# The second feed-forward in the list schedule, its tiles in the buffers of w_out

## The chip, the cores and the metric

The kernel runs on one core of a Trainium2 chip, as one launch. The metric is the device time of that launch in microseconds. Engines are named as the profile names them: PE is TensorE (PEld its weight loads), DVE VectorE, ACT ScalarE, POOL GpSimd, SP SyncE, which here issues all DMAs.

## What is computed

Windowed attention (4 sequences of 576 tokens, 8 heads of 64, window 64), then a feed-forward with squared ReLU, then a second one with a softmax-weighted activation and a layer norm without bias. The attention's output is 2304 tokens of width 512.

```python
def _moe_ref(x, w_in, w_out):                  # 512 -> 2048 -> 512
    h = np.maximum(x @ w_in, 0.0)
    return (h * h @ w_out).astype(np.float32)

def _moe2_ref(x, w_in, w_out, g_ln):           # 512 -> 1024 -> 512
    h = x @ w_in
    e = np.exp(h - np.max(h, axis=-1, keepdims=True))
    solu = h * (e / (np.sum(e, axis=-1, keepdims=True) + 1e-09))
    mu, var = np.mean(solu, axis=-1, ...), np.mean((solu - mu) ** 2, axis=-1, ...)
    ln = (solu - mu) / np.sqrt(var + 1e-06) * g_ln
    return (ln @ w_out).astype(np.float32)
```

## The kernel before

Every fp32 operand of the large products is split into a high and a low part that TensorE takes, and a product is three matmuls per block (`TERMS`, line 22). The weights arrive as 64-bit floats and are taken apart by DVE and ACT (`weights`, lines 196 to 240).

The first part (lines 175 to 524) works through the tokens in five passes of 8, 6, 8, 6 and 8 blocks of 64 (`PASSES`, line 124). Each pass needs the attention of its blocks, which is spread over the pass before it, and goes through 16 chunks of the 2048 hidden columns. Of chunk kk a pass does a product of 12 matmuls into one bank of `ps_a` (`product`, line 402, in the rows `ps_h L402`), then relu and square on ACT, the exact square on POOL, the low part on DVE (`rest`, line 418, the tile `g`), and 12 matmuls that add the chunk to the pass's sums (`second`, line 428, `ps_y`). The sums of 512 tokens fill four banks: two tiles of `ps_b`. I write y14 and y15 for the last two of these accumulations in the last pass. Behind them DVE and ACT copy the sums out (lines 449 and 451), and SP stores them to `x2_dram`. In the last pass the 16 weight tiles of the second feed-forward replace those of w_in one by one.

The order of all engines in this part is made ahead by `Plan` (lines 25 to 90): every step is a task with an engine, an estimated duration, a rank, the tasks it comes after, and the buffers that it takes and gives back. `run` puts next the task that can start first by its estimates, and among those with one start the lowest rank; the tasks are then written out in the order of their planned starts. Each engine works through its own row in that order.

The second part (lines 527 to 618) stands behind the plan and is written in a plain loop, whose order on the engines the framework settles. Of each of 18 tiles of 128 tokens it loads x from `x2_dram` (`load_x`), splits it into high (ACT, line 544) and low (DVE, line 545), does 24 matmuls h = x w_in into a pair of banks of `ps_b` (`mm_h`, line 555), then on DVE the maximum (560), on ACT the exponential (563), on DVE the scaling (567), the statistics (570, 572) and the centring (576), on POOL the root (575). `mm_t` transposes the result on PE (587) and splits it on ACT (588) and DVE (589); `mm_o` does 24 matmuls with the second weights (599), ACT scales the sums (602), SP stores them. I write h(i), transposes(i) and o(i) for these steps of tile i. In the loop o follows h by two tiles and the transposes by one:

```python
        for i in range(NTT + 2):
            if i < NTT:
                mm_h(i)
                ...
            if 0 <= i - 2 < NTT:
                mm_o(i - 2)
            if 0 <= i - 1 < NTT:
                mm_t(i - 1)
```

PSUM has eight banks: `ps_b` two pairs, `ps_a` two, and two of `ps_t` (scores and attention in the first part, transposes in the second).

Of the kernel before, what the change touches and what calls it, by code (L numbers as in the profile page):

```python
# [93 lines left out]
def kernel(  # L94
# [79 lines left out]

    with ExitStack() as c1:
# [14 lines left out]
        plan = Plan({"raw": RAWS, "wm": WMB, "qk": 1, "v": 1, "e": 2, "pt": 1, "t": 2, "b": 2, "a": 2, "r": 2, "g": 3})  # L190
# [334 lines left out]


    with ExitStack() as c2:
        s_p = c2.enter_context(tc.tile_pool(name="s", bufs=2))
# [1 line left out]
        NTT = NT // P  # L530
        sol, lnT, rst = {}, {}, {}
        x2 = {}

        def load_x(i):
            xr = s_p.tile([P, DC, P], F32, tag="xr", name="xr")
            nc.sync.dma_start(out=xr, in_=x2_dram[:, :, i * P : i * P + P])
            x2[i] = xr

        x2s = {}

        def split_x(i):
            xr = x2.pop(i)
            xx = s_p.tile([P, 2, DC, P], F32R, tag="xx", name="xx")
            S.activation(out=xx[:, 0], in_=xr, func=AF.Copy)
            V.tensor_tensor(out=xx[:, 1], in0=xr, in1=xx[:, 0].bitcast(F32), op=ALU.subtract)
            x2s[i] = xx

        def mm_h(i):
            xx = x2s.pop(i)
            ps = ps_b.tile([P, 2, 512], F32, tag="b", name="ps_h2")  # L550
            for hf in range(NH2):
                n = 0
                for c in range(DC):
                    for wi, xi in TERMS:
                        T.matmul(ps[:, hf, :], xx[:, xi, c, :], w2i[hf * DC + c][:, wi, :],  # L555
                                 start=n == 0, stop=n == 3 * DC - 1)
                        n += 1
            h = ps.rearrange("p a b -> p (a b)")
            nmax = s_p.tile([P, 1], F32, tag="nmax2", name="nmax2")
            V.tensor_reduce(out=nmax, in_=h, axis=AX.X, op=ALU.max, negate=True)  # L560
            e = s_p.tile([P, DFF2], F32, tag="e2", name="e2")
            sums = s_p.tile([P, 1], F32, tag="sums2", name="sums2")
            S.activation(out=e, in_=h, func=AF.Exp, bias=nmax, accum_out=sums)
            rs = s_p.tile([P, 1], F32, tag="rs2", name="rs2")
            V.tensor_scalar(out=rs, in0=sums, scalar1=1e-9, scalar2=None, op0=ALU.add)
            V.reciprocal(rs, rs)
            V.scalar_tensor_tensor(out=e, in0=e, scalar=rs, in1=h, op0=ALU.mult, op1=ALU.mult)
            bn = s_p.tile([P, NH2, 6], F32, tag="bn", name="bn")
            for hf in range(NH2):
                V.bn_stats(out=bn[:, hf, :], in_=e[:, hf * 512 : hf * 512 + 512])  # L570
            mv = s_p.tile([P, 2], F32, tag="mv", name="mv")
            V.bn_aggr(out=mv, in_=bn.rearrange("p a b -> p (a b)"))
            rstd = s_p.tile([P, 1], F32, tag="rstd", name="rstd", bufs=4)
            V.tensor_scalar(out=rstd, in0=mv[:, 1:2], scalar1=1e-6, scalar2=None, op0=ALU.add)  # L574
            G.tensor_tensor(out=rstd, in0=rstd, in1=mhalf, op=ALU.pow)  # L575
            V.tensor_scalar(out=e, in0=e, scalar1=mv[:, 0:1], scalar2=None, op0=ALU.subtract)
            sol[i] = e
            rst[i] = rstd

        def mm_t(i):  # L580
            e = sol.pop(i)
            l = s_p.tile([P, 2, KF2, P], F32R, tag="lnT", name="lnT")
            for hf in range(KF2 // 4):
                ps = ps_t.tile([P, 4, P], F32, tag="t", name="ps_lt")
                for u in range(4):
                    kk = 4 * hf + u
                    T.transpose(ps[:, u, :], e[:, kk * P : kk * P + P], ident)  # L587
                S.activation(out=l[:, 0, 4 * hf : 4 * hf + 4, :], in_=ps, func=AF.Copy)  # L588
                V.tensor_tensor(out=l[:, 1, 4 * hf : 4 * hf + 4, :], in0=ps,  # L589
                                in1=l[:, 0, 4 * hf : 4 * hf + 4, :].bitcast(F32), op=ALU.subtract)  # L590
            lnT[i] = l

        def mm_o(i):
            l = lnT.pop(i)
            ps = ps_a.tile([P, 512], F32, tag="a", name="ps_o")
            n = 0
            for kk in range(KF2):
                for wi, xi in TERMS:
# [62 lines left out]
```

## Time and profile before

| | |
|---|---|
| median of three runs | 728.3 us (727.86 to 731.81) |
| the profiled execution | 728.8 us |
| its span, first to last instruction | 726.7 us |
| PE busy | 697.0 us (96%), 4630 instructions |
| PEld busy | 605.5 us (83%) |
| DVE, ACT, POOL busy | 371.5, 307.9, 139.0 us |
| granted PE clock, mean | 0.988 of full speed |

Matmuls overlap each other, so PE's busy time says where it had work, not how fast it went. The pace is read from the start of one group to the start of the next in the chain that ended last, and a stall from the idle time before an instruction in the timeline. The granted clock is 1.00 at 2.4 GHz and 0.50 at 1.2 GHz.

### The profile page before, as it was taken

The page shows a single profiled execution, that of the slowest core. Times are in us where ns is not written, and L with a number is a line of the kernel's source. Part 1 is how long each engine was busy: PE and PEld are TensorE (multiplying, and loading weights), DVE is VectorE, ACT ScalarE, POOL GpSimd, SP SyncE. Part 2 cuts the span into 40 slices and gives each one's busy share as a digit, 9 for nine tenths or more (in the row PEclk, how much of TensorE's full clock was granted, in tenths as well). Part 3 has the DMA queues.
Part 4 walks back from the last instruction along what each step waited for, and adds up shares of the span by engine and source line. Part 5 has one row for each costly group of instructions (what it writes and reads, how often), then busy time and mean ns, then how long its engine had stood idle before and what let it go on. Part 6 is the DMA issues. An engine that isn't in the chain of part 4 may idle for free.

```text
span 726.7 us, 11758 instructions
## 1 busy us (share of the span) xinstructions
PE 697.0 (96%) x4630; PEld 605.5 (83%) x4630; DVE 371.5 (51%) x678; ACT 307.9 (42%) x755; POOL 139.0 (19%) x161
## 2 busy tenths in 40 slices
PE   6687999999999999999999999998999999999997
PEld 3677888999999888788999988886888888888876
DVE  3999999522333221322223166555675646665561
ACT  5776767334445233433434243455323231323132
POOL 2122332412223122222222121121010011010100
PEclk9889999999999999999999999999999999999999
DMA  7766644012222211212111062222211011110001
GB/s 225 252 203 227 212 151 147 31 38 87 66 66 67 73 36 30 63 40 86 39 66 60 1 206 99 89 85 66 80 44 58 30 45 44 59 39 35 14 30 43
DMA packets 34565, 60.51 MB, mean 83 GB/s; under 512 B 5072, under 2 KB 16336, under 8 KB 34512
## 3 DMA queue, kind: packets, MB, share of 16 engines
q1 hardware_dynamic: 34512, 59.78, 24.7%
q8 instruction: 36, 0.59, 0.3%
q14 instruction: 17, 0.14, 0.1%
HBM read 50.34 MB, written 9.44 MB: 82 GB/s over the span
## 4 chain that ended last, share of the span: by engine, by line
PE 81%; DVE 11%; issue 2%; DMA 2%; ACT 2%; SPq 0%; POOL 0%; ACTq 0%; DVEq 0%
PE ps_h L402 24%; PE ps_y L428 23%; PE ps_h L555 14%; PE ps_o L599 14%; DVE wm L215 3%; PE ps_lt L587 2%; DVE wm L220 2%; PE ps_v L350 2%; PE ps_s L294 2%; PE ps_p L327 1%; DVE wm L210 1%; DVE wa L231 1%; DVE g L418 1%; DVE wb L231 1%; DMA qk<-in_k 1%
## 5 line engine op out<-in xcount | busy, mean ns | idle before, releaser
L402 PE MATMUL ps_h<-x,wa 128*128 128x256 f32 (+2 forms) x1152 | 220.5, 344 | 4.3 <-DVE wa L231 2.5
L428 PE MATMUL ps_y<-g,wb 128*128 128x256 f32 (+2 forms) x1152 | 219.6, 343 | 5.2 <-DVE g L418 5.0
L428 PEld LDWEIGHTS ps_y<-g,wb 128*128 128x128 f32 x1152 | 188.2, 190 | 26.2 <-DVE g L418 7.1
L402 PEld LDWEIGHTS ps_h<-x,wa 128*128 128x128 f32 x1152 | 190.4, 194 | 23.1 <-DVE wa L231 3.4
L415 POOL TENSOR_TENSOR r<-r 128x256 f32<-128x256 f32 (+2 forms) x96 | 84.0, 877 | 305.3 <-ACT g L412 288.3
L418 DVE TENSOR_TENSOR g<-r,g 128x256 fp32r<-128x256 f32 (+2 forms) x96 | 55.0, 580 | 152.0 <-POOL r L415 147.6
L408 ACT ACTIVATE r<-ps_h 128x256 f32<-128x256 f32 (+2 forms) x96 | 46.9, 489 | 157.6 <-PE ps_h L402 153.4
L555 PE MATMUL ps_h<-w2i,xx 128*128 128x512 f32 x432 | 104.9, 393 | 0.4 <-ACT y L449 0.4
L599 PE MATMUL ps_o<-w2o,lnT 128*128 128x512 f32 x432 | 104.5, 391 | 0.8 <-ACT lnT L588 0.5
L599 PEld LDWEIGHTS ps_o<-w2o,lnT 128*128 128x128 f32 x432 | 80.7, 188 | 17.9 <-ACT lnT L588 0.8
L555 PEld LDWEIGHTS ps_h<-w2i,xx 128*128 128x128 f32 x432 | 79.9, 188 | 17.0 <-ACT y L449 0.8
L309 ACT ACTIVATE e<-e,nmax 128x128 f32<-128x128 f32 (+1 forms) x144 | 55.0, 384 | 38.4 <-DVE nmax L305 38.4
L602 ACT ACTIVATE o<-ps_o,rstd 128x512 f32<-128x512 f32 x18 | 12.4, 689 | 111.8 <-PE ps_o L599 109.9
L575 POOL TENSOR_TENSOR rstd<-rstd,mhalf 128x1 f32<-128x1 f32 x18 | 16.8, 935 | 192.5 <-DVE rstd L574 192.5
L412 ACT ACTIVATE g<-r 128x256 fp32r<-128x256 f32 (+2 forms) x96 | 50.3, 524 | 5.1 <-PE ps_y L428 2.3
L318 POOL TENSOR_TENSOR e<-e,sums 128x512 f32<-128x512 f32 (+1 forms) x36 | 37.0, 1031 | 73.2 <-DVE sums L315 61.9
L560 DVE TENSOR_REDUCE nmax<-ps_h 128x1 f32<-128x1024 f32 x18 | 21.9, 1218 | 43.9 <-PE ps_h L555 43.9
L301 DVE SCALAR_TENSOR_TENSOR e<-ps_s,mask 128x512 f32<-128x512 f32 (+1 forms) x36 | 23.5, 653 | 38.9 <-PE ps_s L294 38.9
L589 DVE TENSOR_TENSOR lnT<-ps_lt,lnT 128x512 fp32r<-128x512 f32 x36 | 23.3, 683 | 36.3 <-ACT lnT L588 36.3
L220 DVE SCALAR_TENSOR_TENSOR wm<-wraw,wm 128x512 int32<-128x512 int32 x48 | 36.3, 757 | 1.2
L215 DVE SCALAR_TENSOR_TENSOR wm<-wraw,wm 128x512 int32<-128x512 int32 x48 | 35.1, 731 | 1.3
L206 ACT ACTIVATE wm<-wraw 128x512 f32<-128x512 f32 x48 | 31.5, 664 | 2.3 <-DMA wraw<-in_w_out 1.7
(57 smaller groups left out, 511.9 us busy)
## 6 DMA issues: line engine op xcount, KB each, us to landing
wraw<-in_w_in SPq DMA_DIRECT2D x24, 512.0 KB, 3.8
wraw<-in_w_out SPq DMA_DIRECT2D x24, 512.0 KB, 3.3
vt<-in_v SPq DMA_DIRECT2D x32, 256.0 KB, 2.9
kt<-in_k SPq DMA_DIRECT2D x16, 384.0 KB, 4.2
xr<-x_dram SPq DMA_DIRECT2D x18, 256.0 KB, 3.1
out<-o SPq DMA_DIRECT2D x18, 256.0 KB, 2.0
qt<-in_q SPq DMA_DIRECT2D x17, 256.0 KB, 2.8
x_dram<-y SPq DMA_DIRECT2D x12, 256.0 KB, 2.5
```

Source lines behind the costliest of these rows:

```text
L215: V.scalar_tensor_tensor(out=t, in0=o["raw"][:, :, 1], scalar=-0x80000000, in1=t, op0=ALU.bitwise_and, op1=ALU.bitwise_or)
L220: V.scalar_tensor_tensor(out=t, in0=o["raw"][:, :, 0], scalar=29, in1=t, op0=ALU.logical_shift_right, op1=ALU.bitwise_or)
L309: S.activation(out=o["er"][:, a, w], in_=o["er"][:, a, w], func=AF.Exp, bias=o["nmax"][:, a, w : w + 1], accum_out=o["sums"][:, a, w : w + 1])
L318: G.tensor_tensor(out=o["er"][:, a], in0=o["er"][:, a], in1=o["sums"][:, a].unsqueeze(2).to_broadcast([P, HP, W]), op=ALU.mult)
L402: T.matmul(ps[:, :N], wa[kk][:, wi, c * P : c * P + P], xs[t][:, xi, c, n0:n1], start=n == 0, stop=n == 3 * DC - 1)
L408: S.activation(out=o["r"], in_=o["h"][:, :N], func=AF.Relu)
L412: S.activation(out=o["g"][:, 0, :N], in_=o["r"], func=AF.Square)
L415: G.tensor_tensor(out=o["r"], in0=o["r"], in1=o["r"], op=ALU.mult)
L418: V.tensor_tensor(out=o["g"][:, 1, :N], in0=o["r"], in1=o["g"][:, 0, :N].bitcast(F32), op=ALU.subtract)
L428: T.matmul(acc[t][d // 2][:, d % 2, n0:n1], wb[kk][:, wi, d * P : d * P + P], o["g"][:, xi, :N], start=kk == 0 and n == 0 and n0 == 0, sto ...
L555: T.matmul(ps[:, hf, :], xx[:, xi, c, :], w2i[hf * DC + c][:, wi, :], start=n == 0, stop=n == 3 * DC - 1)
L599: T.matmul(ps, l[:, xi, kk, :], w2o[kk][:, wi, :], start=n == 0, stop=n == 3 * KF2 - 1)
```

## The change

The second feed-forward's steps become tasks of the plan, in one function per tile (`tile2`), so they share ranks and buffers with the last pass. The arithmetic and the sizes of the instructions are those of before, but for a product h(i), which is planned in two halves of 12 matmuls, and o(i), likewise. Its tiles (x, its split, the exponential, the split transposes, the result) take buffers of `wb_p`, 16 tiles that held w_out and that the last pass gives back one by one (`"wb": 0`, `gone`). The sums of the last pass lie in one tile of `ps_b` and the two banks of `ps_t`, so that a pair of `ps_b` is free for h(0). `x2_dram` becomes one tensor per pass, so that a load of x waits for its own pass's stores only. The last product of the last pass gets a lower rank, and the last tiles' o a higher one. The line numbers of the new program differ: L431 is y, L537 h, L575 the transposes, L590 o, L526 and L529 the split of x, L454 and L456 the copies of the sums.

```diff
-    x2_dram = dram.tile([P, DC, NT], F32, name="x2_dram")
+    x2_dram = [dram.tile([P, DC, n * BLK], F32, name=f"x2_dram{t}") for t, n in enumerate(PASSES)]
...
-        plan = Plan({..., "r": 2, "g": 3})
+        plan = Plan({..., "r": 2, "g": 3, "wb": 0})
...
-                    acc[t] = [ps_b.tile([P, 2, 512], F32, tag="b", name="ps_y") for _ in range(2)]
+                    acc[t] = [ps_b.tile([P, 2, 512], F32, tag="b", name="ps_y") for _ in range(1 if t == LAST else 2)]
+                    acc[t] = [a[:, i] for a in acc[t] for i in range(2)]
+                    if t == LAST:
+                        acc[t] += [ps_t.tile([P, 512], F32, tag="t", name="ps_y") for _ in range(2)]
...
-            i = add("PE", mm(N), rank, product, [ready["a", kk], *done], take=["a"])
+            i = add("PE", mm(N), rank - 6 * (last and t == LAST), product, [ready["a", kk], *done], take=["a"])
...
-            p = add("PE", mm(N), rank + 4.5, second, [e, ready["b", kk], before], take=["b", "b"] if first else [], give=["g"])
+            gone = ["wb"] * (t == LAST)
+            p = add("PE", mm(N), rank + 4.5, second, [e, ready["b", kk], before], take=[] if not first else ["b", "t", "t"] if t == LAST else ["b", "b"],
+                    give=["g", *gone])
...
+        def spare(dtype, name):
+            return wb_p.tile([P, 2, 512], dtype, tag="wb", name=name)
+
+        def tile2(i, rank, rank_o):
...
+            a = add("SP", 1.0, rank - 14, load_x, stored[t] + h_of.get(i - 3, []), take=["wb"], late=2.0)
+            a = add("ACT", 0.62, rank - 6, x_high, [a], take=["wb"])
+            a = add("DVE", 0.62, rank - 6, x_low, [a], port=True, give=["wb"])
+            for hf in range(NH2):
+                a = add("PE", mm(512), rank, lambda hf=hf: mm_h(hf), [a, *(ready["2i", hf * DC + c] for c in range(DC))],
+                        take=["b"] * (hf == 0), give=["wb"] * (hf == 1))
+            h_of[i] = [a]
+            a = add("DVE", 1.17, rank, max_h, [a])
+            a = add("ACT", 1.33, rank, exp_h, [a], take=["wb"])
+            a = add("DVE", 1.45, rank, solu, [a], give=["b"])
+            a = add("DVE", 1.50, rank, stats, [a])
+            r = add("POOL", 1.05, rank, root, [a])
+            a = add("DVE", 0.62, rank, centered, [a], port=True)
+            p = add("PE", 0.95, rank + 6, transposes2, [a], take=["t", "t"], give=["wb"])
+            ls = []
+            for hf in range(2):
+                a = add("ACT", 0.60, rank, lambda hf=hf: t_high(hf), [p], take=["wb"])
+                ls.append(add("DVE", 0.66, rank, lambda hf=hf: t_low(hf), [a], give=["t"]))
+            for hf in range(2):
+                a = add("PE", mm(512), rank_o, lambda hf=hf: mm_o(hf),
+                        [a if hf else None, ls[hf], *(ready["2o", 4 * hf + c] for c in range(4))], take=["a"] * (hf == 0), give=["wb"])
+            a = add("ACT", 0.72, rank_o, scaled, [a, r], take=["wb"], give=["a"])
+            add("SP", 1.0, rank_o, store_o, [a], late=2.0, give=["wb"])
+
+        NTT, TILE = NT // P, 4 * mm(512) + 1.2
+        for i in range(NTT):
+            at = begin[-1] + TILE * i
+            tile2(i, at, at + TILE * (1.5 + 0.6 * max(0, i - (NTT - 5))))
...
-    with ExitStack() as c2:
-        s_p = c2.enter_context(tc.tile_pool(name="s", bufs=2))
-        ps_t = c2.enter_context(tc.tile_pool(name="ps_t2", bufs=2, space=PSUM))
...
```

The order of the engines is the same in both programs up to the last pass. PE before, from the last product of the last pass (L402) over y14 and y15 (L428, 24 in one row) into the second feed-forward:

```order
L402 MATMUL ps_h<-x,wa 128x512 x12
L428 MATMUL ps_y<-g,wb 128x512 x24
L555 MATMUL ps_h_5103<-w2i,xx 128x512 x24
L555 MATMUL ps_h_5151<-w2i,xx 128x512 x24
L555 MATMUL ps_h_5214<-w2i,xx 128x512 x24
L587 MATMUL ps_lt<-ident,e_5130 128x128 x8
L555 MATMUL ps_h_5305<-w2i,xx 128x512 x21
L599 MATMUL ps_o<-w2o,lnT 128x512
L555 MATMUL ps_h_5305<-w2i,xx 128x512 x3
L599 MATMUL ps_o<-w2o,lnT 128x512 x23
L587 MATMUL ps_lt<-ident,e_5178 128x128 x8
```

PE now, the same place:

```order
L402 MATMUL ps_h<-x,wa 128x512 x12
L431 MATMUL ps_y<-g,wb 128x512 x12
L537 MATMUL ps_h_5073<-w2i,xx 128x512 x12
L431 MATMUL ps_y<-g,wb 128x512 x12
L537 MATMUL ps_h_5073<-w2i,xx 128x512 x12
L537 MATMUL ps_h_5130<-w2i,xx 128x512 x24
L537 MATMUL ps_h_5177<-w2i,xx 128x512 x12
L575 MATMUL ps_lt<-ident,e_5147 128x128 x8
L537 MATMUL ps_h_5177<-w2i,xx 128x512 x12
L590 MATMUL ps_o<-w2o,lnT 128x512 x12
L575 MATMUL ps_lt<-ident,e_5197 128x128 x8
L590 MATMUL ps_o<-w2o,lnT 128x512 x36
```

Half of h(0) has moved ahead of y15. Each later h is in two halves with the transposes of the tile before it in between, and o follows at once, a tile earlier than it did; the pattern of four rows (h half, transposes, h half, o) repeats from tile 4 to tile 15.

ACT before, from the last relu and square of the last pass (L408, L412) over the last two weight tiles (L206, L227, L228) to the copies of the sums (L449):

```order
L408 ACTIVATE r<-ps_h 128x512
L412 ACTIVATE g<-r 128x512
L227 ACTIVATE wm<-wm,gcol 128x512
L544 ACTIVATE xx<-xr 128x512
L228 ACTIVATE w2o<-wm 128x512
L206 ACTIVATE wm<-wraw 128x512
L544 ACTIVATE xx<-xr 128x512
L227 ACTIVATE wm<-wm,gcol 128x512
L228 ACTIVATE w2o<-wm 128x512
L449 ACTIVATE y<-ps_y 128x512 x2
```

ACT now, the same place:

```order
L408 ACTIVATE r<-ps_h 128x512
L412 ACTIVATE g<-r 128x512
L227 ACTIVATE wm<-wm,gcol 128x512
L228 ACTIVATE w2o<-wm 128x512
L206 ACTIVATE wm<-wraw 128x512
L227 ACTIVATE wm<-wm,gcol 128x512
L228 ACTIVATE w2o<-wm 128x512
L454 ACTIVATE y<-ps_y 128x512 x2
L549 ACTIVATE e_5147,sums_5148<-ps_h_5073,nmax_5143 128x1024
```

The copies that split x are gone from here; they stand with their DVE halves early in the last pass (tiles 0 to 2) or behind the exponentials.

PE before, the end, from the transposes of tile 15:

```order
L587 MATMUL ps_lt<-ident,e_6424 128x128 x8
L599 MATMUL ps_o<-w2o,lnT 128x512 x13
L587 MATMUL ps_lt<-ident,e_6515 128x128 x4
L599 MATMUL ps_o<-w2o,lnT 128x512 x11
L587 MATMUL ps_lt<-ident,e_6515 128x128 x4
L599 MATMUL ps_o<-w2o,lnT 128x512 x12
L587 MATMUL ps_lt<-ident,e_6604 128x128 x4
L599 MATMUL ps_o<-w2o,lnT 128x512 x12
L587 MATMUL ps_lt<-ident,e_6604 128x128 x4
L599 MATMUL ps_o<-w2o,lnT 128x512 x24
```

PE now, the end, from the transposes of tile 14:

```order
L575 MATMUL ps_lt<-ident,e_6409 128x128 x8
L537 MATMUL ps_h_6437<-w2i,xx 128x512 x12
L537 MATMUL ps_h_6484<-w2i,xx 128x512 x24
L590 MATMUL ps_o<-w2o,lnT 128x512 x12
L575 MATMUL ps_lt<-ident,e_6499 128x128 x8
L590 MATMUL ps_o<-w2o,lnT 128x512 x12
L537 MATMUL ps_h_6584<-w2i,xx 128x512 x12
L575 MATMUL ps_lt<-ident,e_6542 128x128 x8
L537 MATMUL ps_h_6584<-w2i,xx 128x512 x12
L590 MATMUL ps_o<-w2o,lnT 128x512 x36
L575 MATMUL ps_lt<-ident,e_6645 128x128 x8
L590 MATMUL ps_o<-w2o,lnT 128x512 x36
```

The last transposes are no longer split into fours, and o of tiles 14 to 16 is kept back to stand behind the transposes of the next tile.

## Rows read from the trace of the kernel before

**Rows 1.** Stages (us): busy of PE, PEld, DVE, ACT, POOL; clock, DMA, GB/s.

```profile
0.00:100.00 100.00, 79.18 (x807) 67.53 (x808) 85.74 (x169) 69.81 (x207) 25.52 (x39) 0.93 0.64 214
100.00:498.60 398.60, 397.03 (x2793) 355.57 (x2793) 157.68 (x286) 171.28 (x432) 95.61 (x103) 1.00 0.22 71
498.60:508.80 10.20, 7.59 (x25) 5.43 (x23) 5.33 (x10) 5.91 (x10) 1.04 (x1) 0.83 0.40 120
508.80:722.80 214.00, 213.21 (x1008) 176.93 (x1008) 122.73 (x216) 60.22 (x106) 16.83 (x18) 1.00 0.13 43
722.80:726.70 3.90, 0.00 (x0) 0.00 (x0) 0.00 (x0) 0.69 (x1) 0.00 (x0) 0.90 0.18 67
...
703.00:705.00 2.00, 1.24 (x6) 0.65 (x5) 1.23 (x2) 2.00 (x4) 0.00 (x0) 1.00 0.35 131
```

**Rows 2.** The same view, the two stretches behind the gap at the seam.

```profile
504.00:506.00 2.00, 1.95 (x5) 1.57 (x6) 2.00 (x4) 0.27 (x1) 0.00 (x0) 0.51 0.43 125
506.00:508.00 2.00, 2.00 (x7) 1.61 (x6) 1.43 (x3) 1.07 (x2) 0.00 (x0) 0.63 0.44 130
```

**Rows 3.** Timeline of PE at the seam: start, us, instruction, [idle before <-releaser].

```profile
498.63 3.19 PE L428 MATMUL ps_y<-g,wb 128*128 128x512 f32 x13
504.05 4.37 PE L428 MATMUL ps_y<-g,wb 128*128 128x512 f32 x11 [2.23 <-DVE g L418]
508.82 16.60 PE L555 MATMUL ps_h<-w2i,xx 128*128 128x512 f32 x72 [0.40 <-ACT y L449]
```

**Rows 4.** Timeline of the other engines at the seam.

```profile
498.87 7.21 SPq L536 DMA_DIRECT2D xr<-x_dram  x4
...
500.23 1.04 POOL L415 TENSOR_TENSOR r<-r 128x512 f32<-128x512 f32 x1 [4.48 <-ACT g L412]
502.04 0.63 ACT L544 ACTIVATE xx<-xr 128x512 fp32r<-128x512 f32 x1 [1.27 <-DMA xr<-x_dram]
...
502.70 0.69 DVE L545 TENSOR_TENSOR xx<-xr,xx 128x512 fp32r<-128x512 f32 x1 [3.84 <-ACT xx L544]
...
503.31 0.68 DVE L418 TENSOR_TENSOR g<-r,g 128x512 fp32r<-128x512 f32 x1
...
509.06 0.68 DVE L231 TENSOR_TENSOR w2o<-wm,w2o 128x512 fp32r<-128x512 f32 x1
```

**Rows 5.** The chain that ended last: start, us, what.

```profile
493.26 2.79 PE ps_y L428 x12
...
537.19 0.87 PE ps_lt L587 x8
...
549.64 4.80 PE ps_h L555 x21
...
573.24 4.80 PE ps_h L555 x21
```

**Rows 6.** Timeline of DVE in the first tiles of the second feed-forward.

```profile
514.58 1.23 DVE L560 TENSOR_REDUCE nmax<-ps_h 128x1 f32<-128x1024 f32 x1 [4.83 <-PE ps_h L555]
...
517.46 1.28 DVE L567 SCALAR_TENSOR_TENSOR e<-e,rs,ps_h 128x1024 f32<-128x1024 f32 x1
...
532.09 1.21 DVE L560 TENSOR_REDUCE nmax<-ps_h 128x1 f32<-128x1024 f32 x1
...
538.50 1.29 DVE L589 TENSOR_TENSOR lnT<-ps_lt,lnT 128x512 fp32r<-128x512 f32 x2 [3.64 <-ACT lnT L588]
...
540.47 1.28 DVE L567 SCALAR_TENSOR_TENSOR e<-e,rs,ps_h 128x1024 f32<-128x1024 f32 x1
...
543.42 0.74 DVE L576 TENSOR_SCALAR e<-e,mv 128x1024 f32<-128x1024 f32 x1
```

**Rows 7.** Timeline early in the last pass, PE and ACT.

```profile
426.78 2.95 PE L428 MATMUL ps_y<-g,wb 128*128 128x512 f32 x12
...
432.57 0.60 ACT L408 ACTIVATE r<-ps_h 128x512 f32<-128x512 f32 x1 [0.27 <-PE ps_h L402]
```

**Rows 8.** Timeline of PE, its last instructions.

```profile
717.09 5.70 PE L599 MATMUL ps_o<-w2o,lnT 128*128 128x512 f32 x24
```

More of the change, by code (lines that the diff above doesn't have):

```diff
@@ L127 @@
     ORDER = FIRSTS + [j for j in range(NB) if j % blocks_per_seq]
-    HALF, BEHIND = len(FIRSTS), 6
+    HALF, BEHIND, LAST = len(FIRSTS), 6, len(PASSES) - 1
     assert sum(PASSES) == NB and PASSES[0] == 2 * HALF and HALF % 2 == 0
@@ L179 @@
         g_p = c1.enter_context(tc.tile_pool(name="g", bufs=3))
+        s_p = c1.enter_context(tc.tile_pool(name="s", bufs=2))
         ps_t = c1.enter_context(tc.tile_pool(name="ps_t", bufs=2, space=PSUM))
@@ L189 @@
         assert all(n % 2 == 0 for n in PASSES) and blocks_per_seq % 2
[L190 removed]
+        plan = Plan({"raw": RAWS, "wm": WMB, "qk": 1, "v": 1, "e": 2, "pt": 1, "t": 2, "b": 2, "a": 2, "r": 2, "g": 3, "wb": 0})
         add = plan.add
@@ L385, in attention @@
             x_ready[n] = add("DVE", 0.65, rank, rest, [h], give=["b" if alone else "t"])
-        acc, in_of, out_of = {}, {}, {}
+        acc, in_of, out_of, stored = {}, {}, {}, {}
         def mm(N):
@@ L448, in evict @@
                         if d % 2:
-                            S.activation(out=y[:, :n1], in_=acc[t][d // 2][:, d % 2, :n1], func=AF.Copy)
+                            S.activation(out=y[:, :n1], in_=acc[t][d][:, :n1], func=AF.Copy)
                         else:
-                            V.tensor_copy(y[:, :n1], acc[t][d // 2][:, d % 2, :n1])
+                            V.tensor_copy(y[:, :n1], acc[t][d][:, :n1])
                     def store(d=d):
-                        at = starts[t] * BLK
-                        nc.sync.dma_start(out=x2_dram[:, d, at : at + n1], in_=o["y", d][:, :n1])
-                    y = add("ACT" if d % 2 else "DVE", 0.62, rank, evict, [p] + ys[-1:] * (d % 2), take=["wm"], give=["b"] * (d % 2))
+                        nc.sync.dma_start(out=x2_dram[t][:, d], in_=o["y", d][:, :n1])
+                    y = add("ACT" if d % 2 else "DVE", 0.62, rank, evict, [p] + ys[-1:] * (d % 2), take=["wm"],
+                            give=["t"] if t == LAST and d > 1 else ["b"] * (d % 2))
                     ys.append(y)
-                    add("SP", 1.0, rank, store, [y], late=2.0, give=["wm"])
+                    stored.setdefault(t, []).append(add("SP", 1.0, rank, store, [y], late=2.0, give=["wm"]))
         PAIR0, PAIR = 13.0, 6.6
@@ L524 @@
             plan.emit()
-    with ExitStack() as c2:
-        s_p = c2.enter_context(tc.tile_pool(name="s", bufs=2))
-        ps_t = c2.enter_context(tc.tile_pool(name="ps_t2", bufs=2, space=PSUM))
[L530 to L598, printed above, removed]
-                    T.matmul(ps, l[:, xi, kk, :], w2o[kk][:, wi, :], start=n == 0, stop=n == 3 * KF2 - 1)
-                    n += 1
-            o = s_p.tile([P, DM], F32, tag="o", name="o")
-            S.activation(out=o, in_=ps, func=AF.Copy, scale=rst.pop(i))
-            nc.sync.dma_start(out=out[i * P : i * P + P, :], in_=o)
-        load_x(0)
-        load_x(1)
-        split_x(0)
-        for i in range(NTT + 2):
-            if i < NTT:
-                mm_h(i)
-                if i + 1 < NTT:
-                    split_x(i + 1)
-                if i + 2 < NTT:
-                    load_x(i + 2)
-            if 0 <= i - 2 < NTT:
-                mm_o(i - 2)
-            if 0 <= i - 1 < NTT:
-                mm_t(i - 1)
```

73 lines of the change are left out of this document (70 added, 3 removed).

## The prediction

> **What bounds the kernel now.** I read the stages first. TensorE is the engine that ends last, and its idle time lies in four places [rows 1]: 20.8 us in the first 100 us, 1.6 us in the next 398.6, 2.6 us in the 10.2 us between the two feed-forwards, and 0.8 us in the 214.0 us of the second one. Behind its last matmul come 3.9 us of eviction and store. The order of all engines is the same in both programs until the last pass (its weights' split on VectorE and ScalarE, the first x load on SP's queue), so the 20.8 us and the 1.6 us stay, and so do the last 3.9 us. What can move is the seam and the second feed-forward.
>
> At the seam TensorE starts the accumulation of the last chunk but one (y14) at 498.63 and the first product of the second feed-forward at 508.82 [rows 3]: 10.19 us. Two accumulations take 2.79 us each at the pace before it [rows 5], 5.58 in all, so the seam loses **4.61 us**, more than the 2.6 us of idle time. The rest is the clock: behind the gap the granted clock is 0.51 for 2 us and 0.63 for 2 more [rows 2], the lower level (1.2 GHz) for most of it. That is 2 x 0.49 + 2 x 0.37 = 1.7 us. The cause stands in the queues: y15 waits for VectorE's g, and VectorE stood 3.84 us at the split of x, which waits for ScalarE's copy, which waits for the x load that SP issued at 498.87 and that let ScalarE start at 502.04 [rows 4]. POOL had the square ready at 500.23 + 1.04 = 501.27 [rows 4]; g ran at 503.31 all the same.
>
> The second feed-forward runs at 11.80 us a tile (two periods of the chain are 573.24 - 549.64 = 23.60) [rows 5]. 18 tiles are 212.4 us. It takes from 508.82 to 717.09 + 5.70 = 722.79 [rows 3, 8], 213.97 us: **1.57 us** over the dense time, 0.76 of it idle at 703 to 705 [rows 1], the rest the split transposes of the last tiles.
>
> **The change, part by part.**
>
> *The seam.* By the order, half of h(0) (12 matmuls, half of 24, 2.73 us) now stands between y14 and y15, the other half behind y15. The x splits of tiles 0 to 2 have left this place, so g15 follows POOL's 501.27 and is done near 501.3 + 0.7 = 502.0. TensorE comes to y15 at 498.63 + 2.79 + 2.73 = 504.15: 2.1 us of cover. Behind y15 and the second half, at 504.15 + 2.79 + 2.73 = 509.7, stands h(1), which takes the bank pair of y's first half and so waits for VectorE's and ScalarE's evictions. What those two engines do from g15 to the last eviction took, in the trace, from 503.31 to 509.06 + 0.68 = 509.74 [rows 4], waits included; begun at 501.3 it ends by 507.7. It is hidden by 2 us. The second bank pair is free, since the last pass keeps half its sums in the scores' banks; that is what lets tile 0 start early. So the whole 4.61 us should go: -4.61, and at the least the idle 2.6 if the clock fell without a gap, which no row suggests.
>
> *The x loads and splits in the last pass.* Three loads and three splits now stand in the last pass, with SP's queue waiting ahead of weight loads: the first load for y0's end (its buffer is w_out's first), the second for VectorE's first split. ScalarE's first copy waits for y1, 426.78 + 2.79 = 429.6 [rows 7], and the load has then had 5 us where one took 3.2 (498.87 to 502.04) [rows 4]. Behind it on ScalarE are one weight scaling, one rounding and the relu that ran at 432.57 [rows 7]: 2.9 us for three pieces of some 0.6 to 0.7. The weights that SP holds back are needed only at the seam, 70 us later. Cost 0; if a load were 3 us late the relu would slip and the accumulation behind it might wait 1 us, once. Range 0 to 1.
>
> *The tiles in the steady stretch.* The order is now h(i) first half, transposes(i-1), h(i) second half, o(i-1), for i from 4 to 15. The chain behind a product is: maximum to the start of the scaling 517.46 - 514.58 = 2.88; scaling to the end of the centring 543.42 + 0.74 - 540.47 = 3.69 [rows 6]; with 0.2 before it (h(0) ends near 508.82 + 16.60/3 = 514.35 [rows 3]) and 0.1 behind, 6.9 us. TensorE meanwhile does o (24) and half an h (12): at 11.80 less 0.87 for the transposes [rows 5], 36/48 of 10.93 = 8.20 us. Slack 1.3 us. The maximum must also find VectorE free: the split of the transposes ends 538.50 + 1.29 - 537.19 = 2.6 us after they start [rows 5, 6], and TensorE takes 0.87 + 2.73 = 3.60 from there to the end of h. So 11.80 us a tile as before: 0. In the old order three groups of 24 lay over the same chain, so this slack is much thinner than it was.
>
> *The first and the last tiles.* VectorE has tiles 0 and 1 on top of each other. Followed by hand with the same durations: centring of tile 0 ends at 516.5, maximum of 1 at 517.7, the x split at 518.4, scaling of 1 at 520.8, two splits of tile 0's transposes at 522.1, centring of 1 at 524.5. TensorE comes to the transposes of tile 1 at 509.7 + 5.47 + 2.73 + 0.87 + 2.73 + 2.73 = 524.2: a wait of 0.3. At the end: h(16) ends 5.47 after h(15); its centring follows tile 15's on VectorE and ends some 14.8 after h(15), where TensorE is there at 14.5: 0.3. Transposes of tile 17 have 36 matmuls over their chain (8.2 against 6.9), and o(17) has half of o(16) over its splits. So the 1.57 us of before becomes 0.6: **-1.0**; bounds 0 and -1.57.
>
> *The new buffers.* Tiles of the second feed-forward take w_out's buffers, 16 of them, six a tile. Behind the first three loads and splits, at least 85 matmuls and transposes stand in TensorE's order between the last reader of a buffer and the instruction that takes it; a tile has 56. Cost 0.
>
> **Sum.** -4.61 - 1.57 + 0.6 = -5.6 us. Against the profiled execution, 726.7 of span and 728.8 in all: 721.1 and 723.2. The median of the runs shown is 728.3, 0.5 under the profiled one, so I forecast **722.7 us**, 0.8% less. About 0.5% (3.6 us, 724.7) is what a measurement can tell from no change.
>
> **The rivals.**
>
> *The gain comes in part.* The waits at the transposes of tiles 1 and 16 are short by my reckoning, but either may drop the clock as the gap from 501.82 (498.63 + 3.19) to 504.05 did [rows 3]. Each would cost the 1.7 us of [rows 2], 3.4 for both: 726.1, no measurable change. Against it: the 0.76 us of idle time at 703 to 705 left the clock at 1.00 there [rows 1]. The Trainium skill (TensorE: Matmul & The Clock Gate, A second HAM failure mode: psum-queue depth-cycling) tells of a kernel that cycled PSUM banks and micro-idled so often that its clock kept falling; by that rule the new order, with its thinner slack, would go this way. The trace disagrees so far as it goes: the old second feed-forward cycles the same banks at 1.00 throughout [rows 1]. The same time comes out if a late load or late evictions at the seam give back 3 us. Chance 0.15.
>
> *The chain behind each product is longer than its cover.* The mechanism is the thin slack: if exp stands in ScalarE's queue behind something that waits (an x copy for its load, an o copy for its matmuls), every tile's transposes wait. The trace has it: from the maximum at 532.09 to the end of the centring at 544.16 tile 3 took 12.07 us [rows 6], harmless under the old cover. With 0.3 around it that is 12.4, 4.2 over the 8.20; 12 tiles make 50 us, less 5.6: 773 us. It decides from 1.3 + 5.6/12 = 1.8 us of stretch, and is slower by over 0.5% from 2.1. Against it: in the new order exp stands directly behind the copies of the preceding transposes, which with VectorE's part are done 1 us before the product ends (2.6 against 3.60). Chance 0.05.
>
> **How the numbers follow.** Forecast 0.80 (721.6, no wait at all and half a microsecond of scatter, to 724.6), partial 0.15 (724.7 to 727), slower 0.05. The range 721.4 to 725.6 leaves out the slow rival, the upper half of the partial one and some scatter below. Faster 0.80, same 0.14, slower 0.06 (the rest is scatter of the runs).
>
> **What would show it.** In the profile of the changed kernel: between y14 and y15 12 matmuls of the second feed-forward and no gap over 0.3 us; the granted clock at 1.00 from 498 to the end; 18 tiles at 11.80 with waits of TensorE for the centring of under 1 us in all; the last matmul ends about 717.2. The forecast is wrong if TensorE waits at the transposes in the steady stretch, if y15 or h(1) waits, or if what lies before the last pass has moved.

## The result and the profile after

The changed kernel takes 723.28 us (median of 5 runs, 722.17 to 724.17), the kernel before, run beside it, 729.49 us (727.86 to 731.81): a ratio of 0.9909 [0.9881, 0.9938], 0.6 to 1.2% faster. The forecast was 722.7 us in 721.4 to 725.6. The profiled execution has a span of 720.3 us against 726.7 before, where the working gave 721.1.

The stages of the new trace, cut at the same events as [rows 1] (columns as there: busy time of PE, PEld, DVE, ACT, POOL, then clock, DMA share, GB/s):

```profile
497.90:508.10 10.20, 10.20 (x46) 8.30 (x45) 5.14 (x9) 5.49 (x9) 1.04 (x1) 1.00 0.09 33
508.10:716.50 208.40, 208.30 (x989) 172.95 (x987) 123.77 (x213) 60.42 (x104) 16.98 (x18) 1.00 0.14 44
...
504.00:506.00 2.00, 2.00 (x11) 1.58 (x10) 0.88 (x2) 1.05 (x2) 0.00 (x0) 1.00 0.04 12
506.00:508.00 2.00, 2.00 (x10) 1.67 (x9) 1.01 (x2) 1.09 (x2) 0.00 (x0) 1.00 0.37 137
```

The 10.2 us at the seam, of which TensorE was busy for 7.59 at a mean clock of 0.83 [rows 1], are now busy throughout at 1.00. The two stretches that showed 0.51 and 0.63 [rows 2] show 1.00. From there to the last matmul 0.1 us of idle time is left.

TensorE's timeline at the seam, which answers to [rows 3] (L431 is the accumulation, L537 the first product of the second feed-forward, L575 the transposes):

```profile
497.90 2.96 PE L431 MATMUL ps_y<-g,wb 128*128 128x512 f32 x12
500.69 2.90 PE L537 MATMUL ps_h<-w2i,xx 128*128 128x512 f32 x12
503.43 2.95 PE L431 MATMUL ps_y<-g,wb 128*128 128x512 f32 x12
506.22 11.06 PE L537 MATMUL ps_h<-w2i,xx 128*128 128x512 f32 x48
517.12 1.04 PE L575 MATMUL ps_lt<-ident,e 128*128 128x128 f32 x8
```

No group has a wait behind it. y14, half of h(0), y15, and then the rest of h(0), h(1) and half of h(2) stand edge to edge: from the start of y14 to the transposes of tile 0 are 19.22 us, where 2 x 2.79 and 60 products of the steady pace (5.47 / 24 each) make 19.25.

The other engines there, which answer to [rows 4]:

```profile
499.50 1.04 POOL L415 TENSOR_TENSOR r<-r 128x512 f32<-128x512 f32 x1 [4.48 <-ACT g L412]
500.58 0.69 DVE L418 TENSOR_TENSOR g<-r,g 128x512 fp32r<-128x512 f32 x1 [2.44 <-POOL r L415]
...
505.73 1.28 DVE L456 COPY y<-ps_y 128x512 f32<-128x512 f32 x2
...
506.44 1.09 ACT L454 ACTIVATE y<-ps_y 128x512 f32<-128x512 f32 x2 [1.36 <-DVE y L456]
```

VectorE now stands idle ahead of g15 and follows POOL by 0.04 us (499.50 + 1.04 = 500.54). g15 ends at 501.27, y15 starts at 503.43. The four evictions end at 506.44 + 1.09 = 507.53; h(1) starts about 506.22 + 2.73 = 508.95.

In the chain that ended last (start, us, what), one row of a steady tile and the same row ten tiles later:

```profile
544.54 2.73 PE ps_h L537 x12
...
662.61 2.73 PE ps_h L537 x12
```

That is 118.07 / 10 = 11.81 us a tile; [rows 5] gave 11.80. What the chain of one steady tile has to spare is seen in the timeline of DVE and PE at tile 4 (its centring, then its transposes):

```profile
556.84 0.74 DVE L567 TENSOR_SCALAR e<-e,mv 128x1024 f32<-128x1024 f32 x1
...
558.92 1.04 PE L575 MATMUL ps_lt<-ident,e 128*128 128x128 f32 x8
```

The centring ends at 557.58, TensorE comes at 558.92: **1.34 us of slack** (1.25 to 1.34 at tiles 3 to 15). At tile 16, where two centrings follow each other, the centring ends at 694.48 + 0.74 = 695.22 and the transposes start at 695.38. The products ahead of them, the transposes and TensorE's last group, which answers to [rows 8]:

```profile
692.43 2.88 PE L537 MATMUL ps_h<-w2i,xx 128*128 128x512 f32 x12
695.38 1.07 PE L575 MATMUL ps_lt<-ident,e 128*128 128x128 f32 x8
...
708.02 8.45 PE L590 MATMUL ps_o<-w2o,lnT 128*128 128x512 f32 x36
```

From the start of these 12 products to the transposes are 2.95 us, where the pace is 2.73: TensorE waits 0.22 us for the centring here, which the timeline doesn't mark because the products' modelled ends overlap what follows.

For the experiments I use one length, **M**: from the start of y14 to the end of the last matmul. Before it was 717.09 + 5.70 - 498.63 = 224.16 us [rows 3, 8], now it is 708.02 + 8.45 - 497.90 = 218.57: 5.59 less. The other 0.8 of the 6.4 us that the span lost are 0.1 behind the last matmul and 0.73 ahead of y14, which started at 498.63 before and at 497.90 here. The seven runs below have the code of the new kernel up to g15, or nearly, and start y14 between 498.63 and 499.92, so these 0.73 us are scatter of the beginning and not of the change.

### The profile page after: what moved, and what is told of

The parts are those of the page before. It is cut to its first block, busy times and chain, and to the rows that moved or that the text cites. A ratio compares the mean times of both kernels' runs of the same rounds, so it can differ in the third digit from the quotient of the medians.

```text
span 720.3 us, 11740 instructions
## 1 busy us (share of the span) xinstructions
PE 693.0 (96%) x4630; PEld 602.2 (84%) x4630; DVE 373.4 (52%) x678; ACT 309.6 (43%) x755; POOL 139.6 (19%) x161
## 4 chain that ended last, share of the span: by engine, by line
PE 85%; DVE 10%; issue 2%; DMA 1%; ACT 1%; SPq 1%; DVEq 0%; ACTq 0%
PE ps_y L431 25%; PE ps_h L402 24%; PE ps_h L537 14%; PE ps_o L590 14%; DVE wm L215 2%; PE ps_lt L575 2%; PE ps_v L350 2%; PE ps_s L294 2%; PE ps_p L327 1%; DVE wm L220 1%; PE ps_warm L640 1%; DVE wm L210 1%; DVE wb L231 1%; DVE wa L231 1%; DMA wraw<-in_w_out 1%
## 5 line engine op out<-in xcount | busy, mean ns | idle before, releaser
L402 PE MATMUL ps_h<-x,wa 128*128 128x256 f32 (+2 forms) x1152 | 218.3, 341 | 5.0 <-DVE wa L231 2.9
L431 PE MATMUL ps_y<-g,wb 128*128 128x256 f32 (+2 forms) x1152 | 218.0, 342 | 3.8 <-DVE g L418 3.6
L402 PEld LDWEIGHTS ps_h<-x,wa 128*128 128x128 f32 x1152 | 188.2, 191 | 23.9 <-DVE wa L231 4.0
L431 PEld LDWEIGHTS ps_y<-g,wb 128*128 128x128 f32 x1152 | 187.1, 189 | 24.2 <-DVE g L418 5.2
L408 ACT ACTIVATE r<-ps_h 128x256 f32<-128x256 f32 (+2 forms) x96 | 46.9, 488 | 150.3 <-PE ps_h L402 146.4
L537 PE MATMUL ps_h<-w2i,xx 128*128 128x512 f32 x432 | 104.8, 394 | 0.0
L590 PE MATMUL ps_o<-w2o,lnT 128*128 128x512 f32 x432 | 101.3, 390 | 0.0
L590 PEld LDWEIGHTS ps_o<-w2o,lnT 128*128 128x128 f32 x432 | 80.9, 188 | 16.7
L537 PEld LDWEIGHTS ps_h<-w2i,xx 128*128 128x128 f32 x432 | 80.0, 188 | 16.4
L412 ACT ACTIVATE g<-r 128x256 fp32r<-128x256 f32 (+2 forms) x96 | 50.3, 524 | 5.3 <-PE ps_y L431 2.7
L549 ACT ACTIVATE e<-ps_h,nmax 128x1024 f32<-128x1024 f32 x18 | 20.1, 1118 | 63.1 <-DVE nmax L544 59.8
L579 ACT ACTIVATE lnT<-ps_lt 128x512 fp32r<-128x512 f32 x36 | 19.5, 595 | 37.4 <-PE ps_lt L575 37.4
L206 ACT ACTIVATE wm<-wraw 128x512 f32<-128x512 f32 x48 | 31.6, 663 | 6.2 <-DMA wraw<-in_w_out 3.3
```

Of the source, the lines that this page charges most:

```text
L402: T.matmul(ps[:, :N], wa[kk][:, wi, c * P : c * P + P], xs[t][:, xi, c, n0:n1], start=n == 0, stop=n == 3 * DC - 1)
L408: S.activation(out=o["r"], in_=o["h"][:, :N], func=AF.Relu)
L412: S.activation(out=o["g"][:, 0, :N], in_=o["r"], func=AF.Square)
L431: T.matmul(acc[t][d][:, n0:n1], wb[kk][:, wi, d * P : d * P + P], o["g"][:, xi, :N], start=kk == 0 and n == 0 and n0 == 0, stop=last and n ...
L537: T.matmul(o["h"][:, hf, :], o["xx"][:, xi, c, :], w2i[hf * DC + c][:, wi, :], start=n == 0, stop=n == 3 * DC - 1)
L590: T.matmul(o["o"], o["l", hf][:, xi, kk % 4, :], w2o[kk][:, wi, :], start=kk == 0 and n == 0, stop=kk == KF2 - 1 and n == 2)
```

## Experiments

Three things in the change touch the seam: the x splits have left VectorE's queue ahead of g15, half of h(0) lies between y14 and y15, and half of the last pass's sums lie in the scores' banks. The theory so far made the first two (idle time and clock) the gain, with the banks as what lets tile 0 start early. The rival is that one of them alone does it. Four kernels, run side by side on one chip, take them apart. A run given with a ratio was timed four times; the other four of the seven below are one profiled execution each and are read by M and their rows alone.

**Without the half of h(0) between y14 and y15.** The first products of tiles 0 to 2 wait in the plan for y15:

```diff
...
-  [a, *(ready["2i", hf * DC + c] for c in range(DC))],
+  [a, *(ready["2i", hf * DC + c] for c in range(DC)), out_of[LAST, 0, KF - 1] if i < 3 else None],
...
```

> The changed kernel, but the products of tiles 0 to 2 may only start behind y15, so nothing of the second feed-forward stands between y14 and y15; x loads, splits and banks stay where the change put them. Measured on the stretch from y14's start to the end of the last matmul (218.57 us in the changed kernel, 224.16 before). My theory: the stall of before was the x split in VectorE's queue ahead of g15; with the split gone, g15 is done 0.64 us behind y14's end, so the stretch grows by 0.6 to 219.2 and the granted clock stays at 1.00. Rival: it is the matmuls put between that fill the gap, and without them the 4.6 us come back: 223.2, with the clock falling.

723.04 us (4 runs), 0.9906 [0.9884, 0.9929] of the kernel before. TensorE's timeline of this run:

```profile
499.69 3.19 PE L431 MATMUL ps_y<-g,wb 128*128 128x512 f32 x13
503.12 2.84 PE L431 MATMUL ps_y<-g,wb 128*128 128x512 f32 x11 [0.23 <-DVE g L418]
505.80 13.80 PE L537 MATMUL ps_h<-w2i,xx 128*128 128x512 f32 x60
519.43 1.04 PE L575 MATMUL ps_lt<-ident,e 128*128 128x128 f32 x8
...
709.89 8.45 PE L590 MATMUL ps_o<-w2o,lnT 128*128 128x512 f32 x36
```

From y14 to the first product are 505.80 - 499.69 = 6.11 us, 0.53 over two accumulations, and 19.74 to the transposes of tile 0, 0.52 more than with the half. M is 709.89 + 8.45 - 499.69 = 218.65, only 0.08 more, because the steady tile was 0.03 us shorter in this run (see the last section). So the half of h(0), which the order shows first, is worth half a microsecond here, too little for the times of whole kernels to show (723.04 us against 723.28). With the split gone from the queue, y15 waits 0.23 us for g15 and no more.

**The same, with g15 made late.** Four passes of VectorE over r (1.81 us in all) stand ahead of g15, about the delay that the x split had made:

```diff
...
+ for _ in range(4 * (last and t == LAST)):
+     V.tensor_scalar(out=o["r"], in0=o["r"], scalar1=1.0, scalar2=None, op0=ALU.mult)
```

> As e1_no_fill, and four multiplications by one of 0.42 us each on VectorE ahead of g15, which delay it by 1.7 us, so that TensorE's gap is 2.3 us again as before the change. My theory: the gap itself makes the clock fall, so the stretch grows by 2.3 of waiting and 1.7 of slow clock to 222.6, with a granted clock near 0.5 for some 3 us behind the gap. Rival: the fall of the clock before the change came from something else at the seam (the loads and stores in flight), and only the wait is paid: 220.9.

TensorE's timeline, and below it the stretches of 2 us:

```profile
499.29 3.19 PE L433 MATMUL ps_y<-g,wb 128*128 128x512 f32 x13
504.66 4.29 PE L433 MATMUL ps_y<-g,wb 128*128 128x512 f32 x11 [2.18 <-DVE g L422]
508.74 13.92 PE L539 MATMUL ps_h<-w2i,xx 128*128 128x512 f32 x60
```

```profile
504.00:506.00 2.00, 1.34 (x5) 1.11 (x6) 1.97 (x4) 0.00 (x0) 0.00 (x0) 0.90 0.01 4
506.00:508.00 2.00, 2.00 (x6) 1.54 (x6) 1.86 (x4) 0.94 (x2) 0.00 (x0) 0.50 0.00 0
508.00:510.00 2.00, 2.00 (x8) 1.63 (x7) 1.08 (x2) 1.50 (x3) 0.00 (x0) 0.75 0.71 262
```

This is the old seam made again: a gap of 2.18 us (before 2.23 [rows 3]), and behind it 0.90, 0.50 and 0.75 of the clock. y14 to the first product takes 508.74 - 499.29 = 9.45 us, 3.87 over two accumulations. The clock has 2 x 0.10 + 2 x 0.50 + 2 x 0.25 = 1.7 of it, the idle time the other 2.2. M is 712.96 + 8.45 - 499.29 = 222.12. The rival without a loss of clock falls.

**The same delay, with the half of h(0) in its place:**

> The changed kernel with the half product between y14 and y15 in place, and g15 delayed by the same 1.7 us (four multiplications by one on VectorE). My theory: the half product covers 2.1 us, so nothing is paid: 218.6, clock 1.00. Rival: the cover is used up by something that the trace does not show, and the delay comes out in part: 219 to 220.3.

```profile
499.15 2.96 PE L433 MATMUL ps_y<-g,wb 128*128 128x512 f32 x12
501.94 2.90 PE L539 MATMUL ps_h<-w2i,xx 128*128 128x512 f32 x12
504.67 2.96 PE L433 MATMUL ps_y<-g,wb 128*128 128x512 f32 x12
507.46 11.29 PE L539 MATMUL ps_h<-w2i,xx 128*128 128x512 f32 x48
```

No gap, though this g15 ended at 504.46 by the same trace (503.77 + 0.69), 0.2 us ahead of y15. M is 218.71, 0.14 more than without the delay. The 48 products behind y15 take 0.23 us longer than in the changed kernel (11.29 against 11.06): the first two of h(1) lose 0.21 of it, about 510.3, just behind ScalarE's first copy of the sums, which began at 509.64. So the half of h(0) covers the whole delay of y15, and 0.2 us of it comes out at h(1).

Each of the two cures is thus enough against the long gap. Over two accumulations and the products between them the seam loses 3.87 us with the delay and no half, 0.53 when only the delay goes, 0.2 when only the half comes, and nothing with both.

**All four sums in the old banks.** This needs the order without the half of h(0), since no bank pair is free then:

```diff
- acc[t] = [ps_b.tile([P, 2, 512], F32, tag="b", name="ps_y") for _ in range(1 if t == LAST else 2)]
+ acc[t] = [ps_b.tile([P, 2, 512], F32, tag="b", name="ps_y") for _ in range(2)]
...
- if t == LAST:
-     acc[t] += [ps_t.tile([P, 512], F32, tag="t", name="ps_y") for _ in range(2)]
...
```

> The changed kernel, but the last pass keeps its sums in the two bank pairs of ps_b as before the change, none in the scores' banks. The plan then has no free pair for h(0): y14 and y15 follow each other, and h(0) stands behind the eviction of the first pair. My theory: 0.64 us of waiting for g15, then some 1.7 us in which h(0) waits for ScalarE's copy of the sums, which stands behind the last weight tile: 220.9; if that second wait drops the clock, 222.6. Rival: the banks don't matter beyond the half product, and it costs what e1_no_fill costs, 0.6.

725.2 us (4 runs), 0.9937 [0.9917, 0.9957]:

```profile
499.53 3.19 PE L429 MATMUL ps_y<-g,wb 128*128 128x512 f32 x13
502.95 2.84 PE L429 MATMUL ps_y<-g,wb 128*128 128x512 f32 x11 [0.23 <-DVE g L418]
507.25 13.90 PE L535 MATMUL ps_h<-w2i,xx 128*128 128x512 f32 x60 [1.46 <-ACT y L452]
```

h(0) waits 1.46 us for ScalarE's eviction, since the pair that it takes is y's. y14 to the first product takes 7.72 us, 2.14 over two accumulations and 1.61 more than with the sums in the scores' banks; M is 711.45 + 8.45 - 499.53 = 220.37. In the old kernel, where y15 itself was late, this wait was 0.40 us [rows 3].

Over two accumulations the seam thus loses 4.61 us before, 2.14 without the x splits in front of g15, 0.53 with the banks as well, and nothing with the half of h(0) as well. Taken in this order the parts are worth **2.5, 1.6 and 0.5 us**; in another order they weigh otherwise, as the half of h(0) does with the delay. The first of the three is the difference to the kernel before, which differs in the rest of the change too: no run puts the x splits alone back. That it was the late g15 which made the gap is shown by [rows 4] and by the delay put back.

**The last tiles without their stretched order.** The ranks of the last output halves are those of the other tiles:

```diff
- tile2(i, at, at + TILE * (1.5 + 0.6 * max(0, i - (NTT - 5))))
+ tile2(i, at, at + TILE * 1.5)
```

> The ranks of the last tiles are not stretched: every output half takes rank at + 1.5 tiles, so the end reads h16a t15 h16b o15 h17a t16 h17b o16 t17 o17. Time from the start of y14 to the end of the last matmul (218.57 us with the change as it is). Theory (the chain of splitting, squaring, centring and scaling takes 6.9 us and has to lie under matrix work; here only one half of o, 5.47 us, lies between the last part of h(17) and the transposes of tile 17, and nothing behind them): the transposes of tile 17 wait 1.4 us, and the last output waits some 1.5 us for the two eviction copies of the transposed sums: about 221.4, and 223 if the clock falls in the first gap. Rival (the order of the last tiles is worth nothing, since the matrix work is the same): 218.6.

725.4 us (4 runs), 0.9932 [0.9907, 0.9958]. TensorE at its end:

```profile
712.80 1.06 PE L575 MATMUL ps_lt<-ident,e 128*128 128x128 f32 x8 [1.46 <-DVE e L567]
714.12 0.50 PE L590 MATMUL ps_o<-w2o,lnT 128*128 128x512 f32 x1 [0.25 <-ACT lnT L579]
714.85 5.55 PE L590 MATMUL ps_o<-w2o,lnT 128*128 128x512 f32 x23 [0.22 <-DVE lnT L583]
```

With only one o (5.47 us) over the chain of 6.9 the transposes wait 1.46 us, and the last product 0.47 in two pieces where 1.5 was expected. M is 714.85 + 5.55 - 499.92 = 220.48, 1.9 more. From the transposes of tile 15 to the end this order takes 720.40 - 690.36 = 30.04 us, the changed kernel 716.47 - 688.79 = 27.68: the stretch is worth 2.4 us (M shows 1.9, since the steady tile was 0.03 us shorter in this run too). The clock stayed at 1.00 behind the gap of 1.46 us, so the higher of the two sums, 223, did not come.

**The chain made longer, by one pass over e and, in a second kernel, by three (0.74 us each):**

```diff
  V.tensor_scalar(out=o["e"], in0=o["e"], scalar1=o["mv"][:, 0:1], scalar2=None, op0=ALU.subtract)
+ for _ in range(1):
+     V.tensor_scalar(out=o["e"], in0=o["e"], scalar1=1.0, scalar2=None, op0=ALU.mult)
```

> One more pass of VectorE over e (128x512, 0.74 us) stands at the end of each tile's centring. Time from the start of y14 to the end of the last matmul (218.57 us with the change as it is). Theory (the chain has 1.3 us to spare under the 8.2 us of matrix work of a steady tile, and nothing to spare at tiles 1 and 16, where 5.47 us cover it and two tiles' centrings follow each other): a steady tile stays at 11.81 us, and the transposes of tiles 1 and 16 wait 0.7 to 1.5 us each: 220.0 to 221.5. Rival (the chain already sets the pace of the steady tiles): each of them is longer by 0.74 us, in all 229 or more.

TensorE in three places of this run (tile 1, two steady tiles, tile 16):

```profile
525.72 1.06 PE L577 MATMUL ps_lt<-ident,e 128*128 128x128 f32 x8 [0.90 <-DVE e L569]
...
549.37 1.04 PE L577 MATMUL ps_lt<-ident,e 128*128 128x128 f32 x8
...
561.18 1.03 PE L577 MATMUL ps_lt<-ident,e 128*128 128x128 f32 x8
...
699.09 1.07 PE L577 MATMUL ps_lt<-ident,e 128*128 128x128 f32 x8 [1.52 <-DVE e L569]
```

The steady tile stays at 561.18 - 549.37 = 11.81 us with 0.74 us more of chain. Between the transposes of tiles 0 and 1 are 7.78 us instead of 6.37, between those of 15 and 16 8.04 instead of 6.59: 1.41 and 1.45 more, together 2.86. M is 711.73 + 8.42 - 498.72 = 221.43, 2.86 more, at the upper end of what was expected.

> As the run with one more pass of VectorE over e, with three of them (2.2 us). Time from the start of y14 to the end of the last matmul (218.57 us with the change as it is). Theory (the slack of a steady tile is 1.3 us; what goes over it is paid in each tile): a steady tile takes 11.81 + 0.9 = 12.7 us, so 12 to 14 of them cost 11 to 13 us, and tiles 1, 16 and 17 some 9 more: about 239, with the granted clock at 1.00 in the steady tiles, since each gap is under 1 us. Rival (each of these gaps brings the clock down to half, as the gap of 2.6 us did at the seam of the kernel before): over 250. Second rival (TensorE's pace doesn't hang on this chain, since the list schedule takes other work first): 219 to 222.

```profile
528.54 1.42 PE L577 MATMUL ps_lt<-ident,e 128*128 128x128 f32 x8 [2.37 <-DVE e L569]
...
554.77 1.07 PE L577 MATMUL ps_lt<-ident,e 128*128 128x128 f32 x8 [0.85 <-DVE e L569]
...
709.42 1.06 PE L577 MATMUL ps_lt<-ident,e 128*128 128x128 f32 x8 [0.93 <-DVE e L569]
...
719.30 1.06 PE L577 MATMUL ps_lt<-ident,e 128*128 128x128 f32 x8 [3.33 <-DVE e L569]
```

Each of the tiles 3 to 15 now waits 0.84 to 0.93 us, thirteen waits in all. Twelve of these tiles take 709.42 - 554.77 = 154.65 us, 12.89 each: 1.08 more than 11.81, where 2.2 less the slack gave 0.9. M is 734.60 + 8.43 - 498.63 = 244.40, 25.8 more, against the 239 of the theory. The steady tiles make 13.0 of the 25.8. The first three and the last two tiles make the other 12.8, where 9 were expected, and in these lies most of what the theory had missed: behind the two long gaps the clock fell (columns as above), by the stretches around these rows for 1.7 us each.

```profile
530.00:532.00 2.00, 2.00 (x6) 1.52 (x6) 1.99 (x5) 1.69 (x3) 0.00 (x0) 0.50 0.00 0
...
720.00:722.00 2.00, 2.00 (x9) 1.62 (x8) 1.29 (x2) 1.05 (x2) 0.00 (x0) 0.56 0.03 8
```

In the steady tiles it did not:

```profile
549.00:710.00 161.00, 149.25 (x700) 121.49 (x698) 115.38 (x190) 41.53 (x71) 16.07 (x13) 1.00 0.12 38
```

So the rival with a drop at every gap falls, and so does the one in which TensorE's pace doesn't hang on the chain. The slack of the steady tiles is between 0.74 and 2.2 us by these two runs, and 2.2 - 1.08 = 1.1 by the second. That is the 1.25 to 1.34 us of the changed kernel's rows less the 0.15 us that lie between the end of a centring and transposes that wait for it (here 553.87 + 0.75 = 554.62 to 554.77).

## Why the prediction held, step by step

**The seam: -4.61 predicted, -4.6 measured.** The size was right and the reading of [rows 2 to 4] too: the split in VectorE's queue made the gap, and the gap took 2.2 us of idle time and 1.7 us of clock, as the kernel with the delay put back shows in both numbers; of the remaining 0.7, h(0)'s wait was 0.40 [rows 3]. The cover of g15 is 503.43 - 501.27 = 2.16 us (2.1 predicted). Reckoned from the start of y14, h(1) came after 11.05 us (11.07 predicted) and the evictions ended after 9.63 (9.07 predicted): they had 1.4 us to spare and not 2. The prediction had taken VectorE's last weight split, done at 509.74 [rows 4], for the last eviction; the old trace has that on ScalarE, behind the split, until 509.84 + 0.60 = 510.44:

```profile
509.84 0.60 ACT L449 ACTIVATE y<-ps_y 128x512 f32<-128x512 f32 x1 [1.07 <-DVE w2o L231]
```

With this end the same reckoning gives 9.8 us. What the prediction didn't separate is the weight of the parts. It told the half of h(0) and the departure of the x splits as one step; the runs show that either would have done nearly all of what both do against the gap, and that the half adds 0.5 us once the splits have left. And it named the banks only as what lets tile 0 start early, while without them and without the half 1.6 us would have stayed.

**The x loads and splits in the last pass: 0 predicted, 0 measured.** From the start of y1 to that of y14 the old kernel took 498.63 - 426.78 = 71.85 us [rows 3, 7], the new one 497.90 - 426.06 = 71.84 us. ScalarE did wait for the end of y1 as foreseen, and later for a weight load that stood behind an x load on SP's queue (from the timeline of ACT):

```profile
429.05 0.63 ACT L526 ACTIVATE xx<-xr 128x512 fp32r<-128x512 f32 x1 [0.91 <-PE ps_y L431]
...
436.37 0.66 ACT L206 ACTIVATE wm<-wraw 128x512 f32<-128x512 f32 x1 [1.93 <-DMA wraw<-in_w_in]
...
437.37 0.60 ACT L408 ACTIVATE r<-ps_h 128x512 f32<-128x512 f32 x1 [0.34 <-PE ps_h L402]
```

The relu behind these was still released by TensorE's product, so nobody else waited.

**The steady tiles: 0 predicted, 0.01 us a tile measured.** The slack is 1.25 to 1.34 us in the trace (1.3 predicted), 1.1 of it usable. That it is a real limit, and lies where the prediction put it, is shown by the two kernels with a longer chain: 0.74 us more cost the steady tiles nothing, 2.2 us more cost each of them 1.08. The rival of a chain longer than its cover, put to decide from 1.8 us of stretch, is thus true as a mechanism and did not come into play.

**The first and the last tiles: -1.0 predicted, -1.0 to -1.1 measured, by errors that nearly cancel.** M less two accumulations and 18 tiles of 11.807 (118.07 / 10) leaves 0.46 us, where the prediction had 0.6 and the old kernel 1.57. The 0.6 was two waits of 0.3 us, at tiles 1 and 16. The one at tile 1 is not there: from the 12 products ahead of its transposes (520.76) to the transposes (523.49) are 2.73 us, the pace. The one at tile 16 is, with 0.22 us, and the transposes start 0.16 us behind the centring, as they do where TensorE waits for one. The rest is the modelled end of the last group (8.45 us for 36 products that take 8.20 at the steady pace). That part was in the 1.57 too (5.70 us for 24 products that take 5.47) and could not go. So the step had one wait too many and no term for the end of the last group. The margin at these two tiles is as thin as it said: one more pass of 0.74 us cost 1.41 and 1.45 us there, since two centrings, each with its pass, follow each other.

**The new buffers: 0 predicted.** In the list of what TensorE waited for stands nothing from y14 on, so no buffer that came free late shows there.

**The rival of a partial gain** was to come from waits at tiles 1 and 16 that drop the clock. The one wait there is, 0.22 us at tile 16, left the clock at 1.00, and in the kernel with three more passes the clock held at 1.00 through thirteen gaps of 0.84 to 0.93 us. The Trainium skill (TensorE: Matmul & The Clock Gate, A second HAM failure mode: psum-queue depth-cycling) tells of frequent micro-idles between groups of matmuls that make the clock oscillate. The kernel with three more passes has such an idle in every steady tile, with banks that cycle, and does not show it there; by that rule it would have gone past 250 us.

The absolute time came out 0.6 us above the forecast and the gain 0.6 us above it as well (6.2 against 5.6), because the kernel before measured 729.49 beside it and not 728.3. Neither is beyond the scatter of the medians.

## To carry to other kernels

A gap on the busiest engine can be made in another engine's queue, by a step that waits for a load and has work behind it that is urgent. Here the gap went when that step was moved away, and it went as well when a filler was put in it; with both, the filler added half a microsecond and is insurance against the delay that may come back. So parts of a change that cure the same gap can't be priced one by one and added up. Price such a gap with the clock behind it, read from the stretches of the trace: here 2.2 us of idle time cost 1.7 us more. Before a tighter order is used, set the chain between two products against the matrix work that lies over it, tile by tile: the slack of a steady tile (1.3 us) says nothing of the first and the last ones, where the same order had none.

## What the runs showed of the hardware

From the seam on, the granted clock stayed at 1.00 behind single gaps of 1.46, 1.46 and 1.52 us in three kernels, and behind thirteen of 0.84 to 0.93 us, one in each tile; it fell to half for 3 to 4 us behind those of 2.18, 2.23, 2.37 and 3.33 us. I had expected that a gap of 1.4 us might do it.

The length of a gap doesn't settle it alone. In the first 100 us, where the gaps stand closer together, one gap has both outcomes in kernels whose code is the same there. The gap of 1.58 us ahead of four transposes of the attention, and the stretch behind it, first in the changed kernel and then in the one with three more passes:

```profile
48.13 0.66 PE L327 MATMUL ps_p<-ident,e 128*128 128x128 f32 x4 [1.58 <-POOL e L318]
50.00:52.00 2.00, 2.00 (x10) 1.72 (x9) 1.93 (x4) 1.74 (x7) 0.00 (x0) 0.50 0.22 86
...
48.53 0.66 PE L327 MATMUL ps_p<-ident,e 128*128 128x128 f32 x4 [1.58 <-POOL e L318]
50.00:52.00 2.00, 1.64 (x14) 1.43 (x12) 1.93 (x5) 1.56 (x6) 0.00 (x0) 1.00 0.15 61
```

A gap of 1.89 to 1.95 us some 13 us before it is followed by a fall in five of the nine traces and by none in four.

The steady tile takes one of two lengths, with the same instructions in the same order: 11.81 us in the changed kernel, in the one with fill and delay and in the one with one more pass, and 11.77 us in the other four that keep the chain's length but for the seam or the end (678.89 - 549.38 = 129.51 us for eleven tiles without the fill, 676.99 - 547.11 = 129.88 with it). The 0.03 us lies in the twelve products behind the transposes (2.98 against 3.01 us). It makes 0.4 us over all the tiles, as much as the half of h(0) gives at the seam. No run was made for it, and its cause stays open.
